# Fox attention and two feed-forward stages on one core: late heads emitted from a table of half-step slots, high parts of turned probabilities on ScalarE

## The chip, the cores and the metric

One core of one Trainium2 chip runs the whole program in one launch. The metric is device time in microseconds (us) of one execution, median of several runs; lower is better.

## The reference, cut to what matters

Attention with forget gates over 4 batches, 8 heads, 576 positions and 64 columns a head, then two feed-forward stages on the 2304 tokens of 512 columns.

```python
log_f = np.log(np.clip(f, 0.0001, 1.0)); cum = np.cumsum(log_f, axis=-1)
decay = cum[:, :, :, None] - cum[:, :, None, :]
scores = np.where(causal, -1e9, q @ k.T / 8 + decay)
attn = softmax(scores) ; x = (attn @ v) as [2304, 512]
x = np.square(np.maximum(x @ w_in, 0.0)) @ w_out        # 512 -> 2048 -> 512
h = x @ w2_in ; out = (h - np.tanh(h)) @ w2_out         # 512 -> 2048 -> 512
```

## The kernel before, in words

Numbers are kept in float32 by splitting each operand of a product into a high part (type fp32r) and a low part (the rest); products then have three terms (high x high, low x high, high x low).

**The first feed-forward stage** runs over 8 blocks of 288 tokens (j = 0 to 7). A block has 16 steps (i). A step g = 16 j + i is `h_step` (12 matmuls into the one PSUM bank `hp`, L159; then on ScalarE Relu into `tmp`, L163, and two Squares, L164 and L165; then the low part `gl`, L119) and the `y_step` of the step two before (12 matmuls into `yp`, L175). The next `h_step` writes the same bank `hp`, so it can't start before the Relu of this one has read it. A step is thus two half-steps of TensorE, h and y. Products of attention are put between them.

**Attention.** The 32 heads (u) run beside blocks 0 to 5, since x of batch b is what blocks 2b and 2b + 1 read. Heads 0 to 7 are done in a way of their own. Heads 8 to 15 have their probabilities transposed on TensorE. From head UT = 16 on, the late heads, transposition goes by another way, and this is where the change lies. For one head:

- `load` brings q and k (tile R) and decay rows (part of QB); `prep` makes the high parts QA on ScalarE and QB on GpSimd and the low parts (GpSimd and VectorE).
- `scores(u, t)` for five tiles of query rows, t = 4 to 0 with 576, 448, 320, 192 and 64 keys: products into `s_ps` (L486, L487), on VectorE a masked minimum (L453), on ScalarE Exp with the row sums (L462), on VectorE sum plus 1e-9 and a reciprocal (L466, L467), then the scaling (L473, on GpSimd or VectorE).
- `turn(t)` (L513 to L519) transposes 32 x 32 squares on VectorE into tile T. `put` writes T to DRAM (p_d, L522), `get` reads it back with four DMAs in another order into PTl (L528). The heads share one T, one PTl and one PTh, so each head's `put`, `get`, split and product take turns.
- `split_p` makes the high part PTh from PTl (L108, four instructions of 512, 512, 384 and 256 columns a head) and replaces PTl by the rest (L119, four instructions).
- `pv` multiplies with the split values VH (L561, L564, L566) into `o_ps`; ScalarE copies the upper half (`xt`), VectorE adds (L576). After every second head `store_x` splits x and stores it (L445, L446); `load_x` (L730) loads a block's x from there.

**What sets the order.** The program text emits instructions in some order. `advance` runs the generator of attention piece by piece between half-steps, by the numbers CUT, ENDS and SLK. Up to MARK, the first step of block 2, each engine keeps the order of emission. From there to the start of block 6 a scheduler that simulates the program chooses each engine's order. From block 6 on each engine keeps the order of emission again. On the chip each engine then executes its instructions in this fixed order. All DMAs named here are issued from one queue, SyncE's.

`ENG` says which engine does an operation: pth (the high parts PTh) on GpSimd, ptl0 to ptl3 on VectorE; for late heads l_n0, l_n2 and l_n4 (scaling of tiles 0, 2, 4) on VectorE, l_n1 and l_n3 on GpSimd.

Of the kernel before, what the change touches and what calls it, by code (L numbers as in the profile page):

```python
# [27 lines left out]
XLOAD = 13  # L28
F0 = 18
SLK = (None, 8, 3, 8, 8, None)  # L30
CUT = (25, 44, 61, 2)
MARK = (2, 0)
UT = 16
ENDS = (28, 27, 27, 27, 32, 24)
ENG = {
# [30 lines left out]
def kernel(  # L66
# [31 lines left out]
    def pre(u):  # L98
        return "" if u < UT else "l_"
# [53 lines left out]
    def h_step(i, x, psh, n, j):  # L153
# [3 lines left out]
        ops = [(w, x, k) for w, x in ((wh, xh), (wl, xh), (wh, xl)) for k in range(NK)]  # L157
# [372 lines left out]
    def split_p(a):  # L530
        hi, lo = PT["h"], PT["l"]
        for c in (2 * a, 2 * a + 1):
            s0 = max(0, c - 1)
            rounded(by("pth"), hi[:, :, c, s0:], lo[:, :, c, s0:].bitcast(F32))
            rest(by(f"ptl{c}"), lo[:, :, c, s0:], lo[:, :, c, s0:].bitcast(F32), hi[:, :, c, s0:])

    def pv(u):
# [33 lines left out]
        xt = one.tile([64, 512], F32, tag="xsh", name="xt")
        rounded(nc.scalar, xt, ps[64:128])
        if u < UT:
            nc.vector.tensor_tensor(xs[r, 64:], ps[0:64], xt, ALU.add)
        else:
            nc.vector.tensor_tensor(  # L576
                xs[r, 64:].rearrange("p (s q j) -> p q s j", s=4, q=4),
                ps[0:64].rearrange("p (q s j) -> p q s j", q=4, s=4),
                xt.rearrange("p (q s j) -> p q s j", q=4, s=4), ALU.add,
            )  # L580
        rounded(by(pre(u) + "xs0"), xs[r, 0:64], ps0[0:64, 0:64])
        if e == 1:
            store_x(b, h // 2, xs, 0, S)
# [43 lines left out]
    def attention_late():  # L627
        for k in range(UT + 1, NU + 1):
            now = k < NU
            if now:  # L630
                load_v(k)
                scores(k, 4)
            yield
            if now:
                scores(k, 3)
                turn(4)
            yield
            if k + 1 < NU:
                prep(k + 1)
            prep_v(k - 1)  # L640
            split_p(0)
            if now:
                scores(k, 2)
                turn(3)
            yield
            if k + 2 < NU:
                load(k + 2)
            split_p(1)
            if now:
                scores(k, 1)  # L650
                scores(k, 0)
                turn(2)
            yield
            if now:
                turn(1)
                turn(0)
                put(k)
            pv(k - 1)
            yield
            if now:  # L660
                get(k)
# [24 lines left out]
    def chain():  # L686
        yield from first_b()
        steady_init()
        load(H)
        yield from attention(H)  # L690
        yield from attention_late()
# [14 lines left out]

    cuts = (0, NB_PIECES + F0, A1 + CUT[3], A1 + CUT[0], A1 + CUT[1], A1 + CUT[2], total)
    PACE = [(cuts[k], cuts[k + 1], ENDS[k]) for k in range(6)]

# [15 lines left out]
    def load_x(j):  # L725
        b, c = divmod(j * TB, S)
        assert all((b, m, S) in STORED for m in range(NK))
        xs = [f1.tile([128, NK, TB], F32R, tag="xhl", bufs=4, name="xhl") for _ in range(2)]
        for a, x in enumerate(xs):
            nc.sync.dma_start(x.bitcast(F32), x_d[b][:, :, a, c:c + TB].rearrange("k p n -> p k n"))  # L730
        return xs
# [204 lines left out]
    G, Y = {}, {}  # L936
    for g in range(NB * NF + LAG):
# [3 lines left out]
        if j < NB:  # L941
            if i == 0 and j == NB - 2:
                advance(total)
                next(ga, None)
# [4 lines left out]
                second_part = {x.name for x in nc.cur_bb.bb.instructions}  # L949
                psh2 = ctx.enter_context(tc.tile_pool(name="psh2", bufs=1, space=bass.MemoryType.PSUM))  # L950
# [4 lines left out]
            piece = cnt[0] - 1 - SLK[j] if j < len(SLK) and SLK[j] is not None else None  # L955
            with tc.issue_after(PEI[piece]) if piece in PEI else ExitStack():
                G[g] = h_step(i, X[j], psh, TB, j)
# [3 lines left out]
            if i == (8 if j == NB - 2 else XLOAD) and j + 1 < NB:  # L961
                X[j + 1] = load_x(j + 1)
# [330 lines left out]
    for chain in ([by_name[n] for n in order if n in first_part], [x for x in emitted if x.name not in second_part]):  # L1293
# [54 lines left out]
```

## Time and profile before

| what | value |
|---|---|
| median of 3 runs (lowest to highest) | 1032.33 us (1032.02 to 1035.81) |
| the profiled execution: its own time | 1036.73 us |
| the profiled execution: span from first to last instruction | 1034.9 us |
| busy share of the span: TensorE, its weight loads, VectorE, ScalarE, GpSimd | 95%, 89%, 72%, 57%, 39% |
| mean granted TensorE clock | 0.995 |
| chain that ended last, by engine | TensorE 65%, VectorE 14%, DMA 11%, ScalarE 5% |

Block 2 starts at 270.8 us of the span, block 6 at 555.1 us; the two blocks without attention end at 661.2 us, and the second feed-forward stage fills the rest. In the profile PE is TensorE's matmul, PEld its weight load, DVE is VectorE, ACT is ScalarE, POOL is GpSimd and SP is SyncE. Starts are in us from the start of the span. A duration in the timeline reaches from an instruction's first to its last work; neighbours on TensorE overlap, so what one costs there is read from start to start.

### The profile page before, as it was taken

How to read it: one execution, taken by the hardware profiler on the slowest of the kernel's cores; microseconds unless marked ns; L12 is line 12 of the kernel's file. 1: busy time of each engine (PE TensorE's matmuls, PEld its weight loads, DVE VectorE, ACT ScalarE, POOL GpSimd, SP SyncE). 2: the span in 40 equal slices, each digit the busy share in tenths (PEclk: the TensorE clock that was granted, in tenths of full speed). 3: DMA queues.
4: the chain of work that ended last, by engine and by line, in shares of the span. 5: the costliest groups of instructions: out<-in, count | busy, mean ns of one | idle time of the engine just before them, and what ended most of it. 6: DMA issues, size and time to landing. Idle time of an engine off the chain costs nothing.

```text
span 1034.9 us, 19719 instructions
## 1 busy us (share of the span) xinstructions
PE 985.8 (95%) x7008; PEld 921.4 (89%) x7008; DVE 747.2 (72%) x1843; ACT 586.4 (57%) x1314; POOL 402.4 (39%) x485
## 2 busy tenths in 40 slices
PE   4989999999999998999999999999999999999998
PEld 3677678888988888898999999998999999999998
DVE  5897776777878877777733667568787788877851
ACT  6886677666645555555545777546565553333330
POOL 4244455555455435335321446437475530000000
PEclk9999999999999999999999999999999999999999
DMA  7655753222946545755526986796877599435451
GB/s 241 205 157 171 192 173 127 85 84 87 319 150 216 201 173 190 254 170 178 187 100 220 342 318 215 303 379 222 300 243 290 194 359 367 149 92 155 142 159 66
DMA packets 86738, 211.55 MB, mean 204 GB/s; under 512 B 8592, under 2 KB 33232, under 8 KB 84336
## 3 DMA queue, kind: packets, MB, share of 16 engines
q1 hardware_dynamic: 86640, 210.29, 59.5%
q8 instruction: 55, 0.90, 0.4%
q14 instruction: 43, 0.35, 0.1%
HBM read 132.21 MB, written 78.05 MB: 203 GB/s over the span
## 4 chain that ended last, share of the span: by engine, by line
PE 65%; DVE 14%; DMA 11%; ACT 5%; issue 3%; SPq 2%; POOL 1%; DVEq 0%; POOLq 0%; ACTq 0%
PE wp L1089 16%; PE yp L175 12%; PE hp L159 12%; PE wp L1013 12%; DMA PTl<-p_d 4%; PE o_ps L564 3%; DMA p_d<-T 2%; PE wp L1101 2%; DMA g_d<-gq 2%; PE o_ps L377 2%; DVE PTl L119 2%; DVE P L453 1%; DMA raw<-in_w_dram 1%; PE s_ps L486 1%; DVE QA L119 1%
## 5 line engine op out<-in xcount | busy, mean ns | idle before, releaser
L159 PE MATMUL hp<-xhl,w 128*128 128x288 f32 x1536 | 235.9, 299 | 6.2 <-ACT tmp L163 5.5
L159 PEld LDWEIGHTS hp<-xhl,w 128*128 128x128 f32 x1536 | 214.5, 189 | 12.4 <-ACT tmp L163 7.1
L175 PE MATMUL yp<-gh,w 128*128 128x288 f32 x1024 | 199.3, 300 | 0.0
L1013 PE MATMUL wp<-xo,wg 128*128 128x288 f32 x1152 | 161.2, 297 | 3.8 <-DVE gq L1020 3.0
L175 PEld LDWEIGHTS yp<-gh,w 128*128 128x128 f32 x1024 | 160.4, 190 | 1.2 <-issue 0.4
L1089 PE MATMUL wp<-go,wg 128*128 128x256 f32 x1344 | 161.4, 283 | 0.0
L1089 PEld LDWEIGHTS wp<-go,wg 128*128 128x128 f32 x1344 | 161.4, 189 | 0.0
L1013 PEld LDWEIGHTS wp<-xo,wg 128*128 128x128 f32 x1152 | 155.5, 189 | 6.3 <-DVE gq L1020 5.3
L175 PE MATMUL yp<-gl,w 128*128 128x288 f32 x512 | 132.9, 299 | 2.8 <-POOL gl L119 1.8
L106 ACT ACTIVATE go<-gt 128x1792 fp32r<-128x1792 f32 (+1 forms) x34 | 58.3, 1717 | 101.4 <-PE wp L1089 79.5
L163 ACT ACTIVATE tmp<-hp 128x288 f32<-128x288 f32 x128 | 51.9, 405 | 112.1 <-PE hp L159 107.1
L462 ACT ACTIVATE P<-P,ST 128x320 f32<-128x320 f32 (+4 forms) x151 | 84.6, 561 | 46.3 <-DVE ST L453 45.2
L119 DVE TENSOR_TENSOR gl<-tmp,gh 128x288 fp32r<-128x288 f32 x96 | 60.2, 628 | 57.5 <-ACT tmp L165 57.2
L473 POOL TENSOR_SCALAR P<-P,ST 128x448 f32<-128x448 f32 (+4 forms) x88 | 60.5, 689 | 96.4 <-DVE ST L467 57.8
L175 PEld LDWEIGHTS yp<-gl,w 128*128 128x128 f32 x512 | 90.6, 190 | 5.2 <-POOL gl L119 2.3
L119 DVE TENSOR_TENSOR go<-gt,go 128x1792 fp32r<-128x1792 f32 (+1 forms) x34 | 69.6, 2047 | 35.4 <-ACT go L106 32.3
L119 POOL TENSOR_TENSOR wt<-wt,whi 128x512 f32<-128x512 f32 (+1 forms) x48 | 60.3, 1276 | 63.1 <-DVE wt L813 33.8
L453 DVE CUSTOM_DVE_ANT_0 P<-s_ps,mk 128x320 f32<-128x320 f32 (+3 forms) x151 | 63.1, 433 | 24.8 <-PE s_ps L487 14.7
L119 DVE TENSOR_TENSOR PTl<-PTl,PTh 128x512 fp32r<-128x512 f32 (+1 forms) x64 | 49.4, 801 | 24.5 <-POOL PTh L108 24.5
L108 POOL TENSOR_SCALAR PTh<-PTl 128x512 fp32r<-128x512 f32 (+1 forms) x64 | 45.3, 732 | 38.5 <-DMA PTl<-p_d 38.4
L164 ACT ACTIVATE gh<-tmp 128x288 fp32r<-128x288 f32 x128 | 56.7, 443 | 3.3
L165 ACT ACTIVATE tmp<-tmp 128x288 f32<-128x288 f32 x128 | 56.4, 441 | 2.9
(160 smaller groups left out, 1726.1 us busy)
## 6 DMA issues: line engine op xcount, KB each, us to landing
raw<-in_w_dram SPq DMA_DIRECT2D x64, 512.0 KB
wg<-wg_d SPq DMA_DIRECT2D x24, 896.0 KB
g_d<-gq SPq DMA_DIRECT2D x32, 576.0 KB
p_d<-T SPq DMA_DIRECT2D x16, 1024.0 KB
PTl<-p_d SPq DMA_DIRECT2D x64, 256.0 KB
gt<-g_d SPq DMA_DIRECT2D x32, 512.0 KB
R<-in_qk_dram SPq DMA_DIRECT2D x24, 576.0 KB
xhl<-x_d SPq DMA_DIRECT2D x14, 576.0 KB
```

Source lines behind the costliest of these rows:

```text
L106: eng.activation(out, in_, AF.Copy)
L119: eng.tensor_tensor(out, in_, hi.bitcast(F32), ALU.subtract)
L159: nc.tensor.matmul(ps, w[:, k * 128:(k + 1) * 128], x[:, k], start=(jj == 0), stop=(jj == 11))
L163: nc.scalar.activation(tmp, ps, AF.Relu)
L164: nc.scalar.activation(gh, tmp, AF.Square)
L165: nc.scalar.activation(tmp, tmp, AF.Square)
L175: nc.tensor.matmul(yp[m][:, :n], w[:, c], x, start=(at == 0 and j == 0), stop=(at == NF - 1 and j == 2))
L453: nc.vector.tensor_tensor_reduce(p[:rows, a:b], ps[:rows, :b - a], mk[:rows, o:o + b - a], -0.125, 3.0e38 if mn is None else mn, ALU.add, ...
L462: nc.scalar.activation(p[:rows, :n], p[:rows, :n], AF.Exp, bias=mn, scale=-1.0, accum_out=st[:rows, 1, t:t + 1])
L473: by(n_by).tensor_scalar(p[:rows, :n], p[:rows, :n], st[:rows, 3, t:t + 1], 1.0, ALU.mult, ALU.mult)
L1013: nc.tensor.matmul(ps, wg[:, ws, k * 128:(k + 1) * 128], xo[:, xs, k], start=(i == 0 and first_), stop=(i == 5), skip_group_check=True)
L1089: nc.tensor.matmul(ps, wg[:, ws, m * 128:(m + 1) * 128], YO[n][xs][:, YX[xn]], start=(j == 0 and m == 0 and i == 0), stop=(j == 2 and i == ...
```

## The change: what it does

1. From block 2 on each engine keeps the order of emission (the last chain now covers all that isn't in the first part); the scheduler chooses nothing there any more.
2. Late heads 17 to 31 are no longer emitted by a generator. `plan_head` puts each head's operations into a table by half-step: head k begins at slot o = START + int(7.75 (k - 17)), with START = -4 (slot 0 is the h of block 2's first step). So heads begin 7 or 8 half-steps apart (7 from head 17 to 18, 21 to 22, 25 to 26 and 29 to 30, else 8), and the last head's output is made in slot 119 of 128. Scores stand in o to o + 3, `turn` in o + 4 and o + 5, `put` in o + 5, `get` in o + 7, the split of the head before in o + 4 and o + 5, its product in o + 5 and o + 6.
3. The high parts PTh (pth) move from GpSimd to ScalarE. The scaling of tiles 0 and 2 moves from VectorE to GpSimd.
4. Sum plus 1e-9 and reciprocal are done for two tiles and for three at once: four small VectorE instructions a head for ten.
5. In `pv` of late heads the products with the high parts come first, those with the low parts after; the nine products are emitted in two slots. Scores of tiles 1 and 0 share one bank.
6. Relu, Squares and `gl` of a step are emitted after fixed parts of the slot (`later`), so that attention's operations stand ahead of or between them.
7. During an odd block the next block's x is loaded in two parts (row tiles 0 to 2, then 3); during an even one from block 2 on it is loaded at step 8 and no longer 13; and the first `h_step` of a block takes tiles 0 to 2 first.
8. Block 1's attention ends with ENDS 26 and takes two pieces less.

```diff
-XLOAD = 13
+XLOADS = (((8, 0, 4),), ((11, 0, 3), (13, 3, 4)), ((13, 0, 4),))
-ENDS = (28, 27, 27, 27, 32, 24)
+ENDS = (28, 26)
+PERIOD = 7.75
+START = -4
...
-    "l_n0": "V", "l_n1": "P", "l_n2": "V", "l_n3": "P", "l_n4": "V",
+    "l_n0": "P", "l_n1": "P", "l_n2": "P", "l_n3": "P", "l_n4": "V",
-    "ptr": "V", "pth": "P", "ptl0": "V",
+    "ptr": "V", "pth": "A", "ptl0": "V",
...
+        if u >= UT:
+            seq = [(hi, 0), (hi, 1), (hi, 2), (hi, 3), (None, 4), (lo, 1), (lo, 2), (lo, 3), (lo, 0)]
...
+    def s_sum(u, a, z):
+        st = ST[u]
+        nc.vector.tensor_scalar(st[:, 2, a:z], st[:, 1, a:z], 1e-9, None, ALU.add)
+        nc.vector.reciprocal(st[:, 3, a:z], st[:, 2, a:z])
...
+    def plan_head(k):
+        o = START + int(PERIOD * (k - UT - 1))
...
+            plan(o, s_products, k, 4, behind=True)
+            plan(o + 1, s_min, k, 4)
+            plan(o + 1, s_exp, k, 4)
...
+            plan(o + 4, turn, 3)
+        if old:
+            plan(o + 4, p_high, 0)
...
+            plan(o + 4, p_high, 3)
+            plan(o + 4, p_low, 0)
+            for c in (1, 2, 3):
+                plan(o + 5, p_low, c)
+            plan(o + 5, pv_begin, k - 1, behind=True)
+            plan(o + 6, pv_end, k - 1, behind=True)
...
+            plan(o + 5, turn, 2)
+            plan(o + 5, turn, 1)
+            plan(o + 5, turn, 0)
+            plan(o + 5, put, k)
+            plan(o + 7, get, k)
...
+            if 2 <= j < NB - 2:
+                if len(later) == 3:
+                    later.pop(0)()
+                    later.pop(0)()
+                planned(slot, False)
+                if later:
+                    later.pop(0)()
+                G[g] = h_step(i, X[j], psh, TB, j, later)
+                planned(slot, True)
+                later.pop(0)()
+                planned(slot + 1, False)
+                later.pop(0)()
...
-    for chain in ([by_name[n] for n in order if n in first_part], [x for x in emitted if x.name not in second_part]):
+    for chain in ([by_name[n] for n in order if n in first_part], [x for x in emitted if x.name not in first_part]):
```

**Where the instructions stand now.** First ScalarE's queue in block 2, in the step where a late head's probabilities come back from DRAM. `tmp<-hp` is the Relu that frees the bank of h, `P` the Exp of a tile, `PTh` the high parts. Before:

```order
L462 ACTIVATE P_1582,ST<-P_1582,ST 128x320
L462 ACTIVATE P_1580,ST<-P_1580,ST 128x192
L462 ACTIVATE P_1579,ST<-P_1579,ST 64x64
L163 ACTIVATE tmp<-hp 128x288
L164 ACTIVATE gh<-tmp 128x288
L165 ACTIVATE tmp<-tmp 128x288
```

With the change:

```order
L476 ACTIVATE P_1579,ST<-P_1579,ST 64x64
L166 ACTIVATE tmp<-hp 128x288
L107 ACTIVATE PTh<-PTl 128x4x128 x2
L107 ACTIVATE PTh<-PTl 128x4x96
L107 ACTIVATE PTh<-PTl 128x4x64
L169 ACTIVATE gh<-tmp 128x288
L170 ACTIVATE tmp<-tmp 128x288
L107 ACTIVATE QA<-R 128x1152
L166 ACTIVATE tmp<-hp 128x288
```

The four high parts, which wait for the four DMAs of `get`, now stand between a Relu and its Squares, ahead of the next Relu. In heads whose slot o + 4 is even they stand ahead of both.

Second VectorE's queue where a head's low parts are made and the next head's tiles are turned. Before:

```order
L119 TENSOR_TENSOR PTl<-PTl,PTh 128x4x128
L473 TENSOR_SCALAR P_1582<-P_1582,ST 128x320
L467 RECIPROCAL ST<-ST 128x1
L119 TENSOR_TENSOR PTl<-PTl,PTh 128x4x128
L119 TENSOR_TENSOR PTl<-PTl,PTh 128x4x96
L119 TENSOR_TENSOR QA<-R,QA 64x576
L516 STREAM_TRANSPOSE T<-P_1582 128x3x4x32
L119 TENSOR_TENSOR PTl<-PTl,PTh 128x4x64
L110 COPY xs<-o_ps 64x64
```

With the change:

```order
L530 STREAM_TRANSPOSE T<-P_1584 128x4x4x32
L120 TENSOR_TENSOR PTl<-PTl,PTh 128x4x128
L120 TENSOR_TENSOR gl<-tmp,gh 128x288
L120 TENSOR_TENSOR PTl<-PTl,PTh 128x4x128
L120 TENSOR_TENSOR PTl<-PTl,PTh 128x4x96
L120 TENSOR_TENSOR PTl<-PTl,PTh 128x4x64
L530 STREAM_TRANSPOSE T<-P_1582 128x3x4x32
L530 STREAM_TRANSPOSE T<-P_1580 128x2x4x32
L527 STREAM_TRANSPOSE T<-P_1579 64x2x32
L120 TENSOR_TENSOR QA<-R,QA 64x576
```

The scaling of tile 2 and the many small reciprocals are gone from between them; the last three transposes, after which `put` can go, stand behind all four low parts of the head before.

Third SyncE's queue, one head. Before:

```order
L522 DMA p_d_84<-T 128x2048
L255 DMA VR<-in_v_dram 128x1x320
L528 DMA PTl<-p_d_84 32x4x512 x4
L236 DMA QB<-aug_d 4x1152
L234 DMA R<-in_qk_dram 128x1152
```

With the change:

```order
L269 DMA VR<-in_v_dram 128x1x320
L536 DMA p_d_84<-T 128x2048
L542 DMA PTl<-p_d_84 32x4x512 x4
L248 DMA R<-in_qk_dram 128x1152
L250 DMA QB<-aug_d 4x1152
```

The load of values VR no longer stands between `put` and `get`. In every second head the two stores of x stand there, before and after.

## Rows read from the trace of the kernel before

**Rows 1.** Busy time by engine: blocks 2 to 5, then block 6 (no attention).

```profile
core 0: us, PE busy (x) PEld busy (x) DVE busy (x) ACT busy (x) POOL busy (x), PEclk, DMA share, GB/s
270.80:555.10 284.30, 269.74 (x1867) 253.01 (x1866) 202.57 (x612) 152.11 (x388) 117.51 (x149) 0.99 0.56 193
555.10:606.30 51.20, 51.19 (x384) 51.20 (x385) 31.87 (x58) 37.42 (x83) 23.71 (x20) 1.00 0.81 293
```

**Rows 2.** Timeline, TensorE: start, duration, tiles, form, count.

```profile
450.56 0.40 PE L564 MATMUL o_ps<-PTl,VH 128*128 128x512 f32 x1
450.80 0.34 PE L564 MATMUL o_ps<-PTh,VH 128*128 128x384 f32 x1
...
451.65 0.34 PE L564 MATMUL o_ps<-PTl,VH 128*128 128x384 f32 x1
...
452.07 1.74 PE L159 MATMUL hp<-xhl,w 128*128 128x288 f32 x12
...
455.33 0.43 PE L561 MATMUL o_ps<-PTl,VR 128*64 128x128 f32 x2
455.69 0.50 PE L564 MATMUL o_ps<-PTl,VH 128*128 128x512 f32 x1
456.02 0.28 PE L486 MATMUL s_ps<-QA 128*128 128x256 f32 x1
...
456.67 1.75 PE L159 MATMUL hp<-xhl,w 128*128 128x288 f32 x12
...
459.85 0.31 PE L486 MATMUL s_ps<-QA 128*128 128x320 f32 x1
...
460.51 1.85 PE L159 MATMUL hp<-xhl,w 128*128 128x288 f32 x12
```

**Rows 3.** Waits, TensorE, blocks 2 to 5: total, times, longest.

```profile
PE o_ps L564 <- POOL PTh L108: 8.0, 7, 2.7
PE hp L159 <- ACT tmp L163: 3.3, 4, 1.2
```

**Rows 4.** Groups by line and form, GpSimd, blocks 2 to 5.

```profile
L108 POOL TENSOR_SCALAR PTh<-PTl 128x512 fp32r<-128x512 f32 x30 | 18.3, 626 | 38.5 <-DMA PTl<-p_d 38.4
```

**Rows 5.** Timeline, SyncE and GpSimd: round trips of heads 16, 22, 23 and 31.

```profile
255.98 0.32 SPq L522 DMA_DIRECT2D p_d<-T  x1
...
358.37 0.33 SPq L522 DMA_DIRECT2D p_d<-T  x1
...
369.69 2.55 POOL L108 TENSOR_SCALAR PTh<-PTl 128x512 fp32r<-128x512 f32 x4 [2.62 <-DMA PTl<-p_d]
...
378.72 0.32 SPq L522 DMA_DIRECT2D p_d<-T  x1
...
383.47 2.53 SPq L528 DMA_DIRECT2D PTl<-p_d  x4
...
389.68 2.48 POOL L108 TENSOR_SCALAR PTh<-PTl 128x512 fp32r<-128x512 f32 x4 [2.68 <-DMA PTl<-p_d]
...
516.18 0.32 SPq L522 DMA_DIRECT2D p_d<-T  x1
```

**Rows 6.** Groups, VectorE, blocks 2 to 5: low parts, transposes; one gl.

```profile
L119 DVE TENSOR_TENSOR gl<-tmp,gh 128x288 fp32r<-128x288 f32 x63 | 33.6, 534 | 24.8 <-ACT tmp L165 24.6
L119 DVE TENSOR_TENSOR PTl<-PTl,PTh 128x512 fp32r<-128x512 f32 x31 | 29.7, 979 | 23.8 <-POOL PTh L108 23.8
...
L516 DVE STREAM_TRANSPOSE T<-P 128x384 f32<-128x384 f32 x14 | 8.0, 569 | 0.1
```

**Rows 7.** Timeline, VectorE and GpSimd: a low part while GpSimd idles.

```profile
376.15 0.38 DVE L119 TENSOR_TENSOR PTl<-PTl,PTh 128x256 fp32r<-128x256 f32 x1
...
378.56 0.12 POOL L250 MEMSET ST<- 128x24 f32 x1 [2.65 <-DVE P L473]
```

**Rows 8.** Groups, ScalarE, blocks 2 to 5: two copies of 256 and 576 columns.

```profile
L106 ACT ACTIVATE VH<-VR 128x256 fp32r<-128x256 f32 x15 | 6.1, 405 | 0.0
L106 ACT ACTIVATE xsh<-xs 128x576 fp32r<-128x576 f32 x8 | 5.4, 674 | 2.3 <-DVE xs L576 2.3
```

More of the change, by code (lines that the diff above doesn't have):

```diff
@@ new lines, in corner, with upper, out @@
+        def corner():
+            ps0 = PS0[u] = bank(u, "o0_ps")
+            nc.tensor.matmul(ps0[0:64, 0:64], vr[0:rows, 0], p0, start=True, stop=True)
+        xt = one.tile([64, 512], F32, tag="xsh", name="xt")
+        def upper():
+            rounded(nc.scalar, xt, ps[64:128])
+        def out():
+            if e == 0:
+                XS[0] = two.tile([128, S], F32, tag="xs", name="xs")
+            xs = XS[0]
+            r = slice(64 * e, 64 * e + 64)
+            if u < UT:
+                nc.vector.tensor_tensor(xs[r, 64:], ps[0:64], xt, ALU.add)
+            else:
+                nc.vector.tensor_tensor(
+                    xs[r, 64:].rearrange("p (s q j) -> p q s j", s=4, q=4),
+                    ps[0:64].rearrange("p (q s j) -> p q s j", q=4, s=4),
+                    xt.rearrange("p (q s j) -> p q s j", q=4, s=4), ALU.add,
+                )
+            rounded(by(pre(u) + "xs0"), xs[r, 0:64], PS0[u][0:64, 0:64])
+            if e == 1:
+                store_x(b, h // 2, xs, 0, S)
@@ L585, in steady_init, with pv @@
+        return products, corner, upper, out
+    PS0 = {}
+    def pv(u):
+        products, corner, upper, out = pv_parts(u)
+        products(0, 9)
+        corner()
+        upper()
+        out()
     def steady_init():
@@ L625, in attention @@
                 yield
[L627 to L661, printed above, removed]
+    PLAN = {}
@@ new lines, with s_products @@
+    MN, BANK, PV = {}, {}, {}
+    def s_products(u, t):
+        qa, qb = QA[u], QB[u]
+        ps = None
+        for t, a, b, c in {4: ((4, 0, 320, 0), (4, 320, 576, 0)), 1: ((1, 0, 192, 0), (0, 0, 64, 192))}.get(t, ((t, 0, NKEY[t], 0),)):
+            q0 = Q0[t]
+            if c == 0:
+                ps = bank(u, "s_ps")
+            o = ps[:, c:c + b - a]
+            nc.tensor.matmul(o, qa[:, 0, q0:q0 + 128], qa[:, 1, a:b], start=True, stop=False)
+            nc.tensor.matmul(o, qb[:, 0, q0:q0 + 128], qb[:, 1, a:b], start=False, stop=True)
+            BANK.setdefault((u, t), []).append((o, a, b))
@@ L663, with planned @@
+    def planned(slot, behind):
+        if slot in PLAN:
+            for f, a in PLAN[slot][behind]:
+                f(*a)
     X = {0: [f1.tile([128, NK, TB], F32R, tag="xhl", bufs=4, name="xhl") for _ in range(2)]}
@@ L723, with load_x @@
     NB = NTOK // TB
-    def load_x(j):
+    def load_x(j, m0, m1):
         b, c = divmod(j * TB, S)
[L727 to L731, printed above, removed]
+        assert all((b, m, S) in STORED for m in range(m0, m1))
+        if j not in X:
+            X[j] = [f1.tile([128, NK, TB], F32R, tag="xhl", bufs=4, name="xhl") for _ in range(2)]
+        for a, x in enumerate(X[j]):
+            nc.sync.dma_start(x[:, m0:m1].bitcast(F32), x_d[b][m0:m1, :, a, c:c + TB].rearrange("k p n -> p k n"))
     WRAW, WT, WX, WG = {}, {}, {}, {}
@@ L936 @@
     G, Y = {}, {}
+    later = []
+    for k in range(UT + 1, NU + 1):
+        plan_head(k)
     for g in range(NB * NF + LAG):
@@ L960 @@
                 advance(lo + int((hi - lo) * min(1.0, (2 * i + 1) / end)))
-            if i == (8 if j == NB - 2 else XLOAD) and j + 1 < NB:
-                X[j + 1] = load_x(j + 1)
+            if j == 1:
+                planned(slot, False)
+                planned(slot, True)
+            for at, m0, m1 in (XLOADS[j % 2 if j else 2] if j < NB - 1 else ()):
+                if i == at:
+                    load_x(j + 1, m0, m1)
         jy, iy = divmod(g - LAG, NF)
```

164 lines of the change are left out of this document (114 added, 50 removed), and 4 rows, old and new, of the table ENG.

## The prediction

> **What bounds the kernel now.** I read the page first: the chain that ended last is 65% TensorE, and TensorE is busy in nine tenths or more of nearly every slice, so only time in which TensorE doesn't run at full pace can be won. Then the table of stretches [rows 1]. Block 6 has no attention: 384 matmuls in 51.20 us, TensorE busy for 51.19 of it; this is its full pace, 1.60 us for each of the 32 half-steps. Blocks 2 to 5, which the change rewrites, take 284.30 us. The reader is to see what full pace would make of them. Four blocks of steps cost 4 x 51.2 = 204.8. What a late head adds I take from the timeline, from one start to the next [rows 2]. Output products: a product of 512 columns 0.24 (450.56 to 450.80), the last of its kind 0.33 (455.69 to 456.02), three of 384 and 256 columns 0.42 (451.65 to 452.07), one more of 384 columns 0.18 (estimate, from the same three), the 128 columns in plain float32 0.36, the corner 0.2 (estimate, half its columns): 3 x 0.24 + 0.33 + 0.42 + 0.18 + 0.36 + 0.2 = 2.21. Score products: 0.65 for four (456.02 to 456.67), 0.66 for six (459.85 to 460.51), and 0.30 for the one remaining pair of 320 columns (estimate): 1.61. With 16 output products and 14 sets of scores in these blocks: 204.8 + 35.4 + 22.5 = 262.7. So **21.6 us** of the 284.3 are TensorE waiting or slowed, and that is all that this change can win there.
>
> The matmul row alone would say less, 284.30 - 269.74 = 14.6 idle, and 1032.33 - 14.6 = 1017.7 as the best possible. [...]
>
> Who makes TensorE wait: output products waiting for high parts from GpSimd, 8.0 us in 7 times, and h waiting for the Relu that frees its bank, 3.3 us in 4 times [rows 3]. GpSimd in turn waited 38.4 us for probabilities to return from DRAM [rows 4].
>
> **The change part by part.** Durations are of the profiled execution, 1036.73 us; the median of the runs is 1032.33, 4.4 less, and I move the difference over unchanged.
>
> *The pace of a late head.* With the table a head has 7 or 8 half-steps. At full pace 8 take 8 x 1.6 + 2.21 + 1.61 = 16.6 us, 7 take 15.0, the mean of 7.75 16.2. Against it stands the round that one head's probabilities hand to the next, since T, PTl and PTh are single. From `put` to the first high part: 389.68 - 378.72 = 10.96 and 369.69 - 358.37 = 11.32 [rows 5]; of the first, 4.75 pass before the first of the four reads is issued. Then, in VectorE's new order: the first high part 0.62 on ScalarE (between 0.405 for 256 columns and 0.674 for 576 [rows 8]); low part, gl, three low parts, three transposes. Low parts cost 0.98 for 512 columns while GpSimd makes high parts beside them [rows 6], but 0.38 for 256 while GpSimd idles (its gap before 378.56 covers 376.15) [rows 7]. With the high parts on ScalarE I take the latter, scaled by columns as an estimate, 0.70, 0.70, 0.55 and 0.40; its upper bound is the 0.98 of now. gl is 0.46 (between 0.43, by columns from the same row, and its mean of 0.534 [rows 6]), the transposes 0.57 [rows 6], 0.4 and 0.2 (estimates by columns). Sum 0.62 + 2.35 + 0.46 + 1.17 = 4.6, so a round is 15.6 to 15.9 us. It fits the 8 half-steps with 0.7 us to spare and lacks 0.6 to 0.9 in the four rounds of 7: 4 x 0.8 = **3.2 us stays**, as a late high part that holds up ScalarE and then h.
>
> *High parts on ScalarE.* Two of 0.62, 0.51 and 0.40 are 2.15 us a head, 16 x 2.15 = 34.4 in the stretch. ScalarE is busy 152.11 of 284.30 [rows 1]; with them 186.5 of about 269, 69%. Hidden by its idle time; the cover is gone in the steps where they stand right ahead of a Relu. There h has 1.6 us (the y between) to lose before TensorE stops. I charge the 3.3 us that h waits for Relu now [rows 3] as **staying**; nothing in the order shortens it.
>
> *VectorE* loses ten small instructions for four, two scalings and the slow low parts; busy 202.57 of 284.30 [rows 1], it isn't the limit, priced at nothing. If the low parts kept what they cost now (0.98 against my 0.70 [rows 6], 40% more, 0.9 a head), a round would be 16.5 to 16.8, and the eleven rounds of 8 half-steps would run late by up to 0.2 as well: 2 us more. *GpSimd* gives 2.5 us a head away [rows 5] and takes two scalings; busy 117.51 of 284.30 [rows 1], nothing. *SyncE's* queue gets six more DMA issues at 0.33 us [rows 5] and is not on the path; `get` still stands behind the two stores of x in every second head, which have 8 half-steps throughout. *x in two parts:* the tightest place is block 6, whose x ends with the last head's output in slot 119, 9 half-steps or 14.4 us ahead. The split (0.67 [rows 8]) and two transfers, store and load, must fit; a read is used 6.2 us after its issue (383.47 to 389.68 [rows 5]), so 13.1 at most. Hidden; if not, some 2 us. *Block 1* keeps its number of pieces per half-step: nothing.
>
> Sum: 21.6 - 3.2 - 3.3 = **15.1 us** less: 1021.6 for an execution like the profiled one, **1017.2** beside the median.
>
> The Trainium skill (ScalarE: Activation LUTs, Rules for kernel authors) speaks against the move to ScalarE: for arithmetic as simple as relu, add and multiply it says VectorE, which is faster per element. By a rate of the Trainium skill (VectorE: DVE Perf Modes, The perf-mode tier table: 2048 float32 values copied in 1.227 us) the 1664 columns of a head would be an estimated 1.0 us on VectorE in place of 2.15. No run here shows it. By the rule a round would be 4.6 - 0.62 + 1.0 = 5.0 beside the trip, 16.0 to 16.3, since the copies would stand in VectorE's own queue, and the sum would be 0.4 x 4 = 1.6 us worse, not better; so I keep the row's 2.15.
>
> **Rivals.**
>
> *1. ScalarE held up by late probabilities (slower).* The 38.4 us that GpSimd waited [rows 4] were mostly harmless: 8.0 reached TensorE [rows 3]. Now ScalarE waits in GpSimd's place, the next Relu behind it, and the one bank of h behind that. If all of it reaches TensorE: 262.7 + 38.4 = 301.1, 16.8 more than now, **1049**. It decides from 21.6 / 15 = 1.4 us of lost TensorE time a head. Against it: the waits come from an order in which GpSimd had nothing else to do, and the table leaves 4 or 5 half-steps between `get` and the high parts. 0.12.
>
> *2. The round sets the pace as before (no change).* From the first `put` to the last, 15 rounds, it takes (516.18 - 255.98) / 15 = 17.35 us a head now [rows 5], more than the 15.6 summed above, so the sum may miss waits that will come back. Then the 120 half-steps of the table, 15.5 rounds, take 268.9, the last 8 half-steps 12.8: 281.7, 2.6 less than now, **1029.7**. For it: the other transfers fall into less time. Against it: now the gaps swing (378.72 - 358.37 = 20.35 is one [rows 5]) in an irregular order, and the table's is regular. 0.16.
>
> *3. All 21.6 go:* **1010.7**, where the DMAs return faster than in the two rounds read. 0.12; it's the lower end of the forecast.
>
> **How the numbers follow.** The forecast, 1011 to 1026 about 1017, has 0.60, rival 3 0.12, rival 2 0.16, rival 1 0.12. A measurement tells about 0.5% (5.2 us) from no change. Faster by more: 0.60 + 0.12 = 0.72; within: rival 2, 0.16; slower: 0.12. The range from 1009 to 1034 takes in rival 3 with some error of the product costs, and rival 2 with 4 us on top; left out are rival 1 and a little at either end, under 0.2.
>
> **What would show it.** Right: blocks 2 to 5 take 266 to 272 us, `put` follows `put` at 15 to 17 us evenly, low parts of 512 columns near 0.7 us, output products wait less than 3 us in all, and h's waits for Relu stay under 8 us, in heads 18, 22, 26 and 30 above all. Rival 1: h waits for Relu 20 us or more, and ScalarE's high parts for DMA. Rival 2: rounds of 17 us. I'm wrong in the frame if the time changes outside blocks 2 to 5 by over 3 us, which nothing above would explain.

## The result, and the profile after

The changed kernel takes 1020.34 us (median of 4 runs, 1017.16 to 1023.18), the kernel before beside it 1032.17 (4 runs, 1030.03 to 1035.81): a ratio of 0.988 with an interval of 0.984 to 0.992. It is faster, by 11.8 us (by the interval, 8 to 17) where the forecast said 15.1 (1017.2). The profiled execution took 1023.18 us, the longest of the four, with a span of 1021.4.

The table of stretches of the changed kernel, cut like [rows 1]: block 1, blocks 2 to 5, block 6.

```profile
core 0: us, PE busy (x) PEld busy (x) DVE busy (x) ACT busy (x) POOL busy (x), PEclk, DMA share, GB/s
...
169.60:266.00 96.40, 95.38 (x651) 86.03 (x650) 68.67 (x234) 64.94 (x166) 52.12 (x74) 1.00 0.33 111
...
266.00:539.90 273.90, 272.63 (x1899) 255.05 (x1898) 184.48 (x512) 184.21 (x461) 101.11 (x125) 1.00 0.58 205
539.90:591.00 51.10, 51.10 (x385) 51.10 (x385) 31.67 (x58) 36.55 (x81) 24.00 (x20) 1.00 0.82 299
```

And block 1 of the kernel before, in the same view:

```profile
166.20:270.80 104.60, 101.70 (x681) 91.47 (x680) 78.36 (x255) 68.34 (x173) 58.30 (x82) 0.98 0.34 116
```

The counts of matmuls come first. Blocks 2 to 5 hold 1899 where [rows 1] has 1867, and block 1 651 where it had 681: the y of block 1's last two steps (24 matmuls, 3.2 us) and a few of attention used to run ahead of block 2's first h and now run behind it, some 4 us in all. Compared with the same work, blocks 2 to 5 went from about 288.3 to 273.9 us, 14.4 less, and block 1 from about 100.6 to 96.4. Both together, 388.9 to 370.3, need no such correction: 18.6 less.

Part of it doesn't show in the total of this pair of executions. Block 0's first h starts at 55.2 us, 4.0 later than before, and the second feed-forward stage takes 375.5 us, 1.8 more. So this pair of executions differs by 13.5 (1036.73 less 1023.18). Neither is put down to the change: in the other thirteen profiles of this study, with the table or without, that h starts at 50.3 to 52.2 us, and over all fourteen that stage takes 369.5 to 376.1, with the same instructions there.

Waits of TensorE in blocks 2 to 5, against [rows 3]:

```profile
PE o_ps L575 <- ACT PTh L107: 0.7, 2, 0.3
PE hp L160 <- DMA xhl<-x_d: 0.4, 1, 0.4
```

Of the 8.0 us for high parts 0.7 are left, and the 3.3 for Relu are gone. Groups of ScalarE and VectorE there, against [rows 4, 6]:

```profile
L107 ACT ACTIVATE PTh<-PTl 128x512 fp32r<-128x512 f32 x32 | 18.4, 624 | 15.3 <-DMA PTl<-p_d 15.2
...
L120 DVE TENSOR_TENSOR gl<-tmp,gh 128x288 fp32r<-128x288 f32 x64 | 34.8, 544 | 21.7 <-ACT tmp L170 21.3
L120 DVE TENSOR_TENSOR PTl<-PTl,PTh 128x512 fp32r<-128x512 f32 x32 | 21.8, 704 | 14.4 <-ACT PTh L107 14.4
L120 DVE TENSOR_TENSOR PTl<-PTl,PTh 128x384 fp32r<-128x384 f32 x16 | 9.3, 583 | 0.0
```

The low part of 512 columns fell from 0.979 to 0.704 us. ScalarE still waits 15.2 us for probabilities to come back. The way of heads 18 and 21 through DRAM, against [rows 5]: SyncE's queue, then ScalarE's first high parts.

```profile
287.78 0.33 SPq L536 DMA_DIRECT2D p_d<-T  x1
291.74 0.33 SPq L459 DMA_DIRECT2D x_d<-xsh  x1
293.26 0.32 SPq L460 DMA_DIRECT2D x_d<-xs  x1
293.68 2.53 SPq L542 DMA_DIRECT2D PTl<-p_d  x4
...
339.79 0.32 SPq L536 DMA_DIRECT2D p_d<-T  x1
...
343.68 2.53 SPq L542 DMA_DIRECT2D PTl<-p_d  x4
```

```profile
301.69 1.56 ACT L107 ACTIVATE PTh<-PTl 128x512 fp32r<-128x512 f32 x3 [1.72 <-DMA PTl<-p_d]
...
352.03 1.15 ACT L107 ACTIVATE PTh<-PTl 128x512 fp32r<-128x512 f32 x2 [1.42 <-DMA PTl<-p_d]
```

In head 18, `get` goes out 5.9 us after `put`, since the two stores of x stand between and the second waits 1.1 us for its low part; in head 21 3.9. From `put` to the first high part it is 13.9 and 12.2 us; the mean over the 16 heads is 12.6.

### The profile page after: what moved, and what is told of

Read it like the earlier page. It is cut to its first block, busy times and chain, and to the rows that moved or that the text cites. A ratio compares the mean times of both kernels' runs of the same rounds, so it can differ in the third digit from the quotient of the medians.

```text
span 1021.4 us, 19668 instructions
## 1 busy us (share of the span) xinstructions
PE 985.0 (96%) x7008; PEld 919.6 (90%) x7008; DVE 718.9 (70%) x1721; ACT 614.5 (60%) x1378; POOL 381.4 (37%) x453
## 4 chain that ended last, share of the span: by engine, by line
PE 74%; DMA 9%; DVE 8%; ACT 4%; issue 2%; SPq 2%; POOL 1%; DVEq 0%; ACTq 0%; POOLq 0%
PE wp L1236 16%; PE yp L189 16%; PE hp L160 15%; PE wp L1160 11%; PE o_ps L575 4%; DMA PTl<-p_d 2%; PE wp L1248 2%; DMA g_d<-gq 2%; PE o_ps L391 2%; DMA R<-in_qk_dram 2%; DMA raw<-in_w_dram 2%; DVE wt L934 1%; DMA p_d<-T 1%; SPq L542 1%; PE t_ps L511 1%
## 5 line engine op out<-in xcount | busy, mean ns | idle before, releaser
L189 PE MATMUL yp<-gh,w 128*128 128x288 f32 x1024 | 213.9, 300 | 0.0
L189 PEld LDWEIGHTS yp<-gh,w 128*128 128x128 f32 x1024 | 164.6, 188 | 2.7 <-issue 1.7
L189 PE MATMUL yp<-gl,w 128*128 128x288 f32 x512 | 151.7, 297 | 1.6 <-POOL gl L120 1.6
L487 POOL TENSOR_SCALAR P<-P,ST 128x192 f32<-128x192 f32 (+4 forms) x120 | 84.0, 707 | 140.5 <-DVE ST L683 84.4
L107 ACT ACTIVATE go<-gt 128x1792 fp32r<-128x1792 f32 (+1 forms) x34 | 58.3, 1717 | 101.3 <-PE wp L1236 73.3
L189 PEld LDWEIGHTS yp<-gl,w 128*128 128x128 f32 x512 | 96.4, 188 | 2.6 <-POOL gl L120 1.8
L120 DVE TENSOR_TENSOR gl<-tmp,gh 128x288 fp32r<-128x288 f32 x96 | 60.8, 635 | 52.7 <-ACT tmp L170 52.2
L1167 DVE TENSOR_TENSOR gq<-wp,sm 128x288 f32<-128x288 f32 x96 | 40.8, 452 | 18.9 <-ACT sm L1166 11.1
L1298 POOL TENSOR_TENSOR gq<-sm,sm 128x288 f32<-128x288 f32 x32 | 28.5, 891 | 59.1 <-ACT sm L1297 36.5
```

What stands on the lines that cost most here:

```text
L107: eng.activation(out, in_, AF.Copy)
L120: eng.tensor_tensor(out, in_, hi.bitcast(F32), ALU.subtract)
L189: nc.tensor.matmul(yp[m][:, :n], w[:, c], x, start=(at == 0 and j == 0), stop=(at == NF - 1 and j == 2))
L487: by(n_by).tensor_scalar(p[:rows, :n], p[:rows, :n], st[:rows, 3, t:t + 1], 1.0, ALU.mult, ALU.mult)
```

## Experiments

Two questions were open: what is left in blocks 2 to 5 (273.9 against a floor of 262.7, with hardly an idle moment), and which part of the change brought the gain. In the table "idle" is a stretch less TensorE's busy time in it; ratios are to the kernel before as it ran beside each (1032.2 to 1035.2 us), with their intervals. A stretch is of one profiled execution. The intervals of most kernels with the table overlap, so these are told apart by their stretches and not by their medians.

| kernel | blocks 2 to 5 | idle | median | ratio |
|---|---|---|---|---|
| before (30 matmuls less there) | 284.3 | 14.6 | 1032.17 | 1 |
| changed | 273.9 | 1.3 | 1020.34 | 0.988 (0.984 to 0.992) |
| e1 no way through DRAM (outputs from old probabilities) | 269.4 | 1.4 | 1015.20 | 0.981 (0.977 to 0.986) |
| e2 high parts on GpSimd | 312.0 | 15.2 | 1051.05 | 1.017 (1.013 to 1.022) |
| e3 scheduler orders | 283.8 (6 less) | 10.6 | 1030.80 | 0.998 (0.994 to 1.001) |
| e4 products in one place | 276.2 | 5.0 | 1016.78 | 0.985 (0.980 to 0.989) |
| e5 get ahead of x stores | 268.5 | 0.1 | 1012.09 | 0.982 (0.979 to 0.985) |
| e6 e4 and e5 | 270.4 | 0.9 | 1015.51 | 0.983 (0.981 to 0.985) |
| e7 PERIOD 7 | 287.0 | 8.8 | 1029.26 | 0.997 (0.995 to 0.999) |
| e8 ENDS 27 | 275.7 | 3.1 | 1020.33 | 0.989 (0.986 to 0.991) |
| e9 scalings on VectorE | 276.5 | 1.9 | 1018.79 | 0.985 (0.979 to 0.991) |
| e10 before, ScalarE | 279.8 (30 less) | 9.5 | 1032.33 | 0.999 (0.996 to 1.003) |
| e11 before, fixed order | 408.4 | 81.6 | 1156.75 | 1.118 (1.113 to 1.123) |
| e12 e5, plain float32 not last | 269.5 | 0.2 | 1013.90 | 0.981 (0.978 to 0.983) |

**What is left above the floor: e1.**

```diff
-            plan(o + 5, put, k)
-            plan(o + 7, get, k)
```

> Leaves out the way through DRAM (put and get) of heads 17 to 31, so their outputs are made from old probabilities; every other instruction stays. It asks what is left above the floor in blocks 2 to 5 of the changed kernel: 273.9 us from block 2's first h to block 6's first h, with TensorE idle for 1.3 of them (273.90 less 272.63), against a floor of 262.7. Theory A, TensorE itself is the bound now and my floor was priced too low (the first h or y matmul behind an output product takes 0.239 us from start to start in place of 0.132): blocks 2 to 5 stay within 272 to 275 us, and the whole within 3 us of the changed kernel. Rival B, late probabilities still slow TensorE in small steps that no wait shows: with nothing to wait for, blocks 2 to 5 fall to 263 to 268 us and the whole by 6 us or more.

```profile
264.10:533.50 269.40, 268.00 (x1898) 254.34 (x1897) 186.86 (x512) 183.12 (x461) 111.24 (x125) 1.00 0.27 90
```

It fell between the two: 269.4, and 1.4 of that is a wait for block 2's x. So about 5 us of the 273.9 hung on the way through DRAM, and 268.0, not 262.7, is what TensorE needs for these products in this order. The list of waits hardly shows those 5 us. In e1 the first block of output products takes 1.2 us from start to start in every head; in the changed kernel it takes 1.7 to 1.8 in six of the 16, since each of its products waits a little behind a matmul still counted as busy. One of the six, with its first four products drawn out to 1.54 us (0.92 in e5, below):

```profile
388.61 1.54 PE L575 MATMUL o_ps<-PTh,VH 128*128 128x512 f32 x4 [0.33 <-ACT PTh L107]
```

e1 also takes away the transfers themselves (DMA share 0.27, for 0.58), so it can't tell late probabilities from traffic.

**Where the 5 us came from: e5.** `get` moves ahead of the output that stores x.

```diff
             plan(o + 7, lambda u: PV[u][2](), k - 1)
-            plan(o + 7, lambda u: PV.pop(u)[3](), k - 1)
...
             plan(o + 7, get, k)
+        if old:
+            plan(o + 7, lambda u: PV.pop(u)[3](), k - 1)
```

> The changed kernel with the four reads of get issued ahead of the two stores of x, where they stand behind them in every second head. Those heads issue get 5.7 to 6.2 us after put (287.78 to 293.68 is one), the others 3.9 (339.79 to 343.68). Theory A, the issue is what makes high parts late there: get comes 3.9 us after put in all heads, and of the 4.4 us that the run without the way through DRAM gained in blocks 2 to 5 (273.8 less 269.4) about half goes: 271 to 272.5 us. Rival B, the transfers are what counts (the stores of x and the load of q and k share the DMA engines with the reads, wherever they are issued): high parts start as long after put as before, 12 to 14 us, and blocks 2 to 5 stay at 273 to 275 us.

SyncE's queue for head 18, the stretch, and ScalarE's group of 512 columns in it:

```profile
281.24 0.33 SPq L536 DMA_DIRECT2D p_d<-T  x1
285.13 2.53 SPq L542 DMA_DIRECT2D PTl<-p_d  x4
287.77 0.54 SPq L459 DMA_DIRECT2D x_d<-xsh  x1
```

```profile
260.10:528.60 268.50, 268.45 (x1899) 254.43 (x1898) 186.82 (x512) 184.07 (x461) 111.67 (x125) 1.00 0.60 208
```

```profile
L107 ACT ACTIVATE PTh<-PTl 128x512 fp32r<-128x512 f32 x32 | 18.4, 623 | 3.5 <-DMA PTl<-p_d 3.2 <-issue 0.2
```

Theory A, and more than it said: 5.4 us went, 0.4 of them the wait for block 2's x, about what e1 had gained. ScalarE's wait for the reads fell from 15.2 to 3.2 us, and the list of TensorE's waits is empty. The traffic is the same here (DMA share 0.60), so it was the order in the queue. e6 and e12, which carry the edit too, take 270.4 and 269.5 us. An edit that changes only this order was worth over a third of what the change itself brought in these blocks. With the shortest stretch it is the version to keep, though its median, 1012.09 us, can't be told from those of e6 and e12.

**The pace of a round: e7.** `PERIOD = 7.75` became 7.

> The changed kernel with PERIOD 7: every late head has 7 half-steps, so attention could end earlier. At full pace such a round takes 7 x 1.6 + 2.75 + 1.7 = 15.7 us. From the trace of the changed kernel the way from put to the first high part takes 12.6 us on average over 16 heads, and from there to the next put 3.9, together 16.5. Theory A, this round of one head's probabilities sets the pace: put follows put at 16.3 us or more, TensorE is idle 6 us or more in blocks 2 to 5, and the whole is 3 to 15 us slower than the changed kernel. Rival B, the high parts come at their time only because their engines' orders make them (the reads were back earlier): put follows put at 15.5 to 16 us, and the whole is within 3 us of the changed kernel or faster.

SyncE's `put` of heads 17 and 31:

```profile
264.93 0.32 SPq L536 DMA_DIRECT2D p_d<-T  x1
...
499.64 0.33 SPq L536 DMA_DIRECT2D p_d<-T  x1
```

Theory A: (499.64 - 264.93) / 14 = 16.77 us a round, though its 7 half-steps need 15.7 (output products waited 5.3 us for ScalarE's high parts, and h 1.9 for the next block's x). In the changed kernel the same 14 rounds take 16.93 each, with e5 16.55. In e7 `get` still stands behind the stores of x; no run has the shorter PERIOD with e5's order, so how short a round could get is open.

**ScalarE or GpSimd, table or scheduler: e2, e3, e10, e11.** e2 sets `"pth": "P"` in the changed kernel, e10 sets `"pth": "A"` in the kernel before. e3 and e11 change the last chain:

```diff
e3:
-[x for x in emitted if x.name not in first_part]
+[x for x in emitted if x.name not in second_part]
e11, in the kernel before:
-[x for x in emitted if x.name not in second_part]
+[x for x in emitted if x.name not in first_part]
```

> The changed kernel with the high parts PTh back on GpSimd; table, order and x loads stay. Theory A, the move to ScalarE is needed with the table: GpSimd's four high parts take 2.5 us a head for ScalarE's 1.87, and VectorE's low parts beside them 0.98 for 0.70, so a round grows by some 1.5 us to over 17 us, more than 7.75 half-steps at full pace hold (16.7): output products wait for GpSimd 5 us or more in all, and the whole is 5 to 15 us slower than the changed kernel. Rival B, the order alone does it and there is room for the slower high parts: within 3 us of the changed kernel, waits of output products under 3 us. Between the two, 3 to 5 us, neither is shown.

> The changed kernel, but in blocks 2 to 5 the scheduler chooses each engine's order again, as in the kernel before; table, engines and x loads stay, so the table only gives the scheduler its priorities. Theory A, the fixed order is what takes the waits away: with the scheduler TensorE's idle time in blocks 2 to 5 comes back to 8 us or more (14.6 before, 1.3 now), and the whole is 6 us or more slower than the changed kernel. Rival B, the table's slots and the engines do it, whoever orders: within 3 us of the changed kernel, idle under 4 us.

> The kernel before with one word changed: the high parts PTh on ScalarE. No table, no fixed order. It completes a square: scheduler or table's order in blocks 2 to 5, high parts on GpSimd or on ScalarE; three corners are measured, 284.3 (scheduler, old emission, GpSimd), 312.0 (table, GpSimd) and 273.8 (table, ScalarE), and 283.8 for the table with the scheduler and ScalarE. Theory A, the move pays only with the table's order: blocks 2 to 5 take 280 to 288 us, the whole within 5 us of before. Rival B, the move alone brings most of the gain: 277 us or less, the whole 7 us or more faster than before. Rival C, ScalarE's late high parts hold up Relu, the first rival of the prediction: 290 us or more.

> The kernel before with the order of emission kept from block 2 on, and nothing else: no table, GpSimd makes the high parts. Theory A, a fixed order pays only with the table, which puts get 4 or 5 half-steps ahead of the high parts: in the generator's order, blocks 2 to 5 take 284 us or more and the whole is not faster than before. Rival B, fixing the order is what brings the gain, whatever the order: 278 us or less, the whole 6 us or more faster than before.

e2, TensorE's waits, VectorE's low parts, then the whole stretch and a slice of it:

```profile
PE o_ps L575 <- POOL PTh L109: 7.8, 13, 1.5
PE o_ps L575 <- DVE PTl L120: 5.9, 9, 0.9
```

```profile
L120 DVE TENSOR_TENSOR PTl<-PTl,PTh 128x512 fp32r<-128x512 f32 x32 | 42.1, 1338 | 31.5 <-POOL PTh L109 31.5
...
L120 DVE TENSOR_TENSOR PTl<-PTl,PTh 128x384 fp32r<-128x384 f32 x16 | 19.3, 1208 | 0.0
```

```profile
262.90:574.90 312.00, 296.77 (x1899) 264.57 (x1898) 210.18 (x512) 157.78 (x397) 130.77 (x189) 0.96 0.51 179
...
520.00:525.00 5.00, 5.00 (x18) 4.07 (x19) 4.97 (x8) 1.06 (x4) 3.10 (x4) 0.50 0.01 5
```

Theory A of e2, at twice its size: 30.7 us slower than the changed kernel, not 5 to 15. I had taken 0.98 us for a low part beside GpSimd; it was 1.34, and a round took 19.4 us (`put` of head 16 at 253.24, of head 31 at 544.04). Of the 38 us that blocks 2 to 5 grew, listed waits are 13.7; a mean granted clock of 0.96 over 312 us makes some 12 more (0.50, that is 1.2 GHz, in all of 520 to 525 us, with TensorE busy throughout, after waits of 1.16 and 0.41 us between 515 and 520). The other 12 stand in no list; waits too short for it are likely, but not shown.

e3 is theory A (idle 10.6, 10.5 us slower than the changed kernel), as are e10, with 279.8 just under its bounds, and e11, though nobody expected some 120 us. So neither half pays alone: ScalarE under the scheduler gains nothing in the whole (0.999, though the one profiled stretch is 4.5 us shorter), the generator's order kept as it is emitted loses 12%, the table with GpSimd loses 1.7%. Together they gain. Points 4 to 7 of the change are in every kernel with the table and were not tried alone.

**Products in one place: e4 and e6.** e4 sets `pv_begin` to slot o + 6; e6 does so in e5.

> The changed kernel with all nine output products of a late head in slot o + 6, where the first five stood in o + 5: one block of output products a head in place of two. Theory A, each block of output products costs the h or y matmul behind it 0.105 us (0.239 for 0.132 from start to start, 32 times): half of them go, 15 x 0.105 = 1.6 us, and blocks 2 to 5 take 272.0 to 272.6 us for 273.9; the whole, by a median that scatters by 3 us, 1019 us. Rival B, that time belongs to the products wherever they stand: within 0.5 us in blocks 2 to 5. Rival C, nine products in one half-step hold up the h behind them, whose Relu then comes late for the next: blocks 2 to 5 take 275 us or more.

> Both edits at once: all nine output products in slot o + 6, and get ahead of the stores of x. With the products in one place alone, blocks 2 to 5 took 276.2 us, of which h waited 5.0 us in 4 times for a Relu behind late high parts, and one of these waits, of 2.3 us, was followed by 2 us at half clock. Theory A, an earlier get makes the high parts come in time: these waits fall under 2 us, and blocks 2 to 5 take 268.5 to 271 us, 3 to 5 less than in the changed kernel; the whole some 1015 us. Rival B, the reads return no earlier, since transfers set the time: waits of h of 4 us or more, 274 us or more.

e4, two slices, and the wait between them:

```profile
345.00:350.00 5.00, 2.72 (x21) 2.49 (x20) 2.57 (x6) 2.52 (x7) 1.22 (x3) 0.99 0.78 273
350.00:355.00 5.00, 5.00 (x22) 4.25 (x20) 3.87 (x7) 1.89 (x4) 2.10 (x3) 0.66 0.53 216
```

```profile
347.48 1.87 ACT L107 ACTIVATE PTh<-PTl 128x512 fp32r<-128x512 f32 x4 [2.48 <-DMA PTl<-p_d]
349.26 0.39 ACT L166 ACTIVATE tmp<-hp 128x288 f32<-128x288 f32 x1
```

```profile
349.70 2.58 PE L160 MATMUL hp<-xhl,w 128*128 128x288 f32 x10 [2.28 <-ACT tmp L166]
```

The clock was at half for some 3.4 us of the second slice (0.66 over 5 us), not for the 2 that e6's expectation names. This is the prediction's first rival, seen: high parts waiting for DRAM stand ahead of a Relu, and the h behind it waits 2.28 us. In the changed kernel output products wait for the same high parts and h doesn't. e4's 276.2 is nominally rival C, but the mechanism is late high parts and not nine products in a half-step: with the earlier `get` (e6) h waits 0.9 us in all, theory A. It is no better than e5, though it has half the blocks of output products; so theory A of e4, 0.105 us for each block, isn't borne out.

**Block 1: e8 and e9.** `ENDS = (28, 27)`; `"l_n0"` and `"l_n2"` on VectorE.

> The changed kernel with block 1's attention spread over 27 half-steps again, as before, in place of 26. Block 1, from its first h to block 2's, took 104.6 us before and 96.2 to 97.2 in the five profiles since; 24 matmuls of y and 6 of attention moved from it to block 2, which explains 4.0 of these 8; the other 4 are a wait of 1.7 us of score products for VectorE at 253.6 us and the 3.5 us at half clock that follow it. Theory A, the earlier end of block 1's attention takes this wait away: with 27 it comes back, and block 1 takes 98.5 us or more. Rival B, it went with the two pieces that left block 1 and the table's new order at its end, not with the 26: block 1 stays at 96 to 97.5 us, and the whole within 3 us of the changed kernel.

> The changed kernel with the scaling of tiles 0 and 2 back on VectorE. The run with 27 half-steps showed that block 1's gain did not come from there. In the trace of before, TensorE's wait in block 1 (1.7 us, score products for VectorE's copy of the corner) stands behind VectorE's scaling of head 16's tile 2, which took 1.97 us for 320 columns at 253.08 while GpSimd was busy too. Theory A, this scaling is the cause: with it back on VectorE block 1 takes 98.5 us or more, where the six profiles with it on GpSimd took 95.6 to 97.2. Rival B, the two pieces that left block 1 took the wait away: 95.5 to 97.5 us. For blocks 2 to 5, where I priced the two scalings at nothing: within 2 us of the changed kernel's 273.8 if that was right, 277 us or more if VectorE's part of the round counts.

Theory A failed both times: block 1 took 95.7 us (0.3 under rival B's bounds) and 96.2. The scaling of head 16's tile 2 before, and in e9:

```profile
253.08 1.97 DVE L473 TENSOR_SCALAR P<-P,ST 128x320 f32<-128x320 f32 x1
```

```profile
251.31 0.39 DVE L487 TENSOR_SCALAR P<-P,ST 128x320 f32<-128x320 f32 x1
```

e10 still has the old order at block 1's end. There the scaling takes 1.98 us again, and TensorE's score products wait behind it, as before:

```profile
251.18 1.98 DVE L473 TENSOR_SCALAR P<-P,ST 128x320 f32<-128x320 f32 x1
```

```profile
253.47 0.39 PE L486 MATMUL s_ps<-QA 128*128 128x256 f32 x1 [1.72 <-DVE xs L110]
```

In both GpSimd makes low parts without a break beside it: first of QB (1.9 us, but it ends 0.3 us after the scaling starts), then of VH and gl. In e9 GpSimd stands idle there. e11 says which point of the change did it. It has the engines, the pieces and the ENDS of before; only the order from block 2 on is fixed. The scaling takes 0.39 us and the wait of 1.7 us is gone:

```profile
250.98 0.39 DVE L473 TENSOR_SCALAR P<-P,ST 128x320 f32<-128x320 f32 x1
```

The low parts of QB and VH no longer stand there, and block 1 takes 101.3 us with a wait of 5.5 for block 2's x in it. So the wait went with point 1, the fixed order, and neither with the 26, nor with the two pieces (rival B of e9), nor with the engine of the scaling. That the low parts beside it are what slows the scaling was not tried alone and stays open.

In blocks 2 to 5 the two scalings on VectorE make a round 17.15 us for 16.93 and the stretch 2.6 us longer, between e9's bounds. That isn't shown to be their price: e8's stretch is 1.8 us longer too, with an edit in block 1 alone, and e9 as a whole is no slower than the changed kernel.

**The floor: e12.** In e5 the products of one block, then the steps around it (start to start):

```profile
330.01 0.92 PE L575 MATMUL o_ps<-PTh,VH 128*128 128x512 f32 x4
330.86 0.43 PE L572 MATMUL o_ps<-PTl,VR 128*64 128x128 f32 x2
331.23 0.54 PE L189 MATMUL yp<-gh,w 128*128 128x288 f32 x2
331.60 0.29 PE L189 MATMUL yp<-gl,w 128*128 128x288 f32 x1
```

Two matmuls of y take 331.60 - 331.23 = 0.37 us right behind the product, 0.26 elsewhere. e12's edit:

```diff
-            seq = [(hi, 0), (hi, 1), (hi, 2), (hi, 3), (None, 4), (lo, 1), (lo, 2), (lo, 3), (lo, 0)]
+            seq = [(hi, 0), (hi, 1), (hi, 2), (None, 4), (hi, 3), (lo, 1), (lo, 2), (lo, 3), (lo, 0)]
...
-        PV[u][0](5, 9)
-        PV[u][1]()
+        PV[u][0](5, 8)
+        PV[u][1]()
+        PV[u][0](8, 9)
```

> The kernel with get ahead of the stores of x, in which TensorE has no wait left in blocks 2 to 5 (268.4 us), with one more edit: of each block of output products the last is now a product in fp32r (the high part of 256 columns; the low part of 512 columns) in place of one in plain float32 (the 128 columns with VR; the corner), which goes one place earlier. Behind a block of output products the first h or y matmul takes 0.237 to 0.239 us from start to start, in place of 0.132; that is 32 x 0.106 = 3.4 us of the 5.7 by which my floor of 262.7 was short. Theory A, the plain float32 product at the end makes it: the matmul behind takes 0.135 us now, and blocks 2 to 5 get 2 to 3.4 us shorter, 265 to 266.5. Rival B, the time belongs to the plain float32 product wherever it stands and now falls on the output product behind it: blocks 2 to 5 stay at 268 to 269 us.

```profile
331.12 0.43 PE L572 MATMUL o_ps<-PTl,VR 128*64 128x128 f32 x2
331.49 0.39 PE L575 MATMUL o_ps<-PTh,VH 128*128 128x256 f32 x1
331.71 0.43 PE L189 MATMUL yp<-gh,w 128*128 128x288 f32 x2
331.97 0.30 PE L189 MATMUL yp<-gl,w 128*128 128x288 f32 x1
```

Rival B: y takes its 0.26 again, but the product of 256 columns between takes 0.22 where it takes 0.12 after another of its kind. The tenth of a microsecond belongs to the plain float32 product, wherever it stands. The stretch takes 269.5 us, half a microsecond over rival B's bounds.

## Why the prediction was right, point by point

The mechanism held: with the table and ScalarE the waits for high parts and Relu went, low parts fell to 0.70 us, and `put` follows `put` evenly at 16.93 us. The number owes something to luck. The 15.1 us were all to come from blocks 2 to 5, which gave 14.4; block 1 gave 4.2 that nobody forecast; and the medians differ by 11.8. By its own sign, 266 to 272 us in blocks 2 to 5, the prediction missed: 273.9, or 269.9 without the 4 us of work that moved in, which it hadn't counted.

- **The floor, 262.7: too low by 5.7.** The step that failed is the cost of output products, 2.21 us a head: from start to start they take 2.33, and 0.105 more for the matmul behind each of their two blocks, 2.54, which is 5.3 of the 5.7; e5, without listed waits, gives 268.4 in all. What hid this is a second slip: the stretch of before, 284.3, held 4 us less work. With both mended the slack was 288.3 - 268.4 = 19.9, not 21.6. The two slips nearly cancel; that was luck.
- **The matmul row or the weight loads.** The Trainium skill (Perfetto Trace Analysis, Identifying the Most-Contended Engine) calls matmul busy time no good measure of how close TensorE is to its roofline, and takes the share of peak arithmetic and the busy time of weight loads instead. The runs agree on the first: in the changed kernel the matmul row leaves 1.3 us where e5 found 5.4. But in e5, with no wait listed, weight loads are busy 254.43 of 268.50 and leave 14.1 us, of which no run here won any. The sum from starts, with a kernel that waits for nothing beside it, was the better measure.
- **3.2 us stay in short rounds, 3.3 for Relu: 5.4 stayed, for another reason.** h waits for Relu nowhere. The step that failed is "`get` still stands behind the two stores of x in every second head, which have 8 half-steps throughout", read as harmless, and SyncE's queue "is not on the path": it was, and e5 shows that 5 of the 5.4 hung on it (the other 0.4 was block 2's x).
- **A round of 15.6 to 15.9 us: 16.8 (e7).** Of its parts, from the first high part to the next `put` (4.6 forecast) was 4.05 in the changed kernel, the low part of 512 columns 0.704 (0.70), of 384 columns 0.583 (0.55), gl 0.544 (0.46); the way from `put` to the first high part was 12.6 and not 11. Two rounds read from before were too few, and short ones: over its 16 heads that way took 13.4 on average. Rival 2, whose sign was rounds of 17 us, thus had the round nearly right, but 7.75 half-steps with their products need 16.6 us anyway, so it cost little: blocks 2 to 5 gained 14.4, not 2.6.
- **ScalarE.** 18.4 us for the columns of 512, 2.06 us a head with the other two (2.15), busy 184.21 of 273.90, 67% (69%). Rival 1 didn't come: h waited for no Relu; e4 shows it when the output products shift, e2 what the other engine would have cost. No run has these copies on VectorE.
- **GpSimd's and VectorE's edits at nothing:** neither confirmed nor refuted; e9's stretch is 2.6 us longer, its whole no slower.
- **Outside blocks 2 to 5:** block 1 gained 4.2 us where I said nothing, the frame's own bound exceeded. The step that failed is "*Block 1* keeps its number of pieces per half-step: nothing": the fixed order from block 2 on also changes what runs at block 1's end (e11). Its wait of 1.7 us stood in the trace, and so did what followed it:

```profile
251.20:256.20 5.00, 3.29 (x19) 2.44 (x18) 4.81 (x8) 2.21 (x6) 3.79 (x6) 0.95 0.35 117
256.20:261.20 5.00, 5.00 (x28) 4.91 (x28) 3.11 (x12) 2.13 (x6) 2.75 (x3) 0.70 0.81 329
...
423.70:428.70 5.00, 2.99 (x22) 2.44 (x20) 2.43 (x7) 2.60 (x10) 1.40 (x3) 1.00 0.91 256
428.70:433.70 5.00, 5.00 (x26) 4.91 (x25) 4.94 (x17) 1.30 (x3) 4.43 (x5) 0.66 0.51 149
```

These are slices of the kernel before, of block 1 and of block 4: twice, after TensorE had stood still for about 2 us, the granted clock fell to half for some 3.5 us, about 1.7 us each time that no list of waits shows. But the longest wait of blocks 2 to 5 in the same trace, 2.7 us for high parts between 387 and 391 us, was followed by no fall:

```profile
388.00:392.00 4.00, 1.65 (x10) 1.34 (x11) 2.07 (x7) 1.70 (x5) 2.32 (x4) 1.00 0.14 51
392.00:396.00 4.00, 4.00 (x27) 3.56 (x26) 3.88 (x8) 1.30 (x3) 4.00 (x4) 1.00 0.01 2
```

## What to carry to other kernels

Before pricing a queue at nothing, read what stands in it between the two ends of a round trip: here a store that waited for its data held up the reads behind it by some 2 us, and the loss showed neither at the store nor in the list of TensorE's waits. Compare stretches only after comparing their instruction counts. And measure a floor with a kernel that waits for nothing, rather than by adding up single products alone.

## What was unexpected of the hardware

- VectorE beside GpSimd slows far more than the rows of before showed: the low part of 512 columns 0.704 us with ScalarE making the high parts, 1.338 with GpSimd; a scaling of 320 columns 0.39 and 1.97 us (in this last pair the cause is not isolated).
- The matmul right behind a plain float32 product takes 0.1 us more, from start to start, be it of y or an output product (e5, e12).
- A wait of TensorE can cost nearly twice its length. After 1.71 and 2.01 us in the kernel before and 2.28 in e4, the granted clock fell to 0.50, that is 1.2 GHz, for some 3.4 us, which loses 1.7; after 1.72 us in e10 and 2.66 in the kernel before it stayed at 1.00. Length alone doesn't decide it, and what does, these runs don't settle.
